# A transformer block on one core: the array's work cut into blocks of two matmuls, and an opening with the identity made on chip

## The chip, the core and the metric

The kernel runs on one core of a Trainium2 chip. The metric is the device time of one execution in microseconds (us), lower is better. The engines are TensorE (PE, "the array"; its weight loads are PEld), VectorE (DVE), ScalarE (ACT), GpSimd (POOL) and SyncE (SP), which issues most DMAs. Each engine takes its instructions in order; they meet through semaphores.

## What is computed

Input x is 2048 x 1024 (S x D), everything in bfloat16. The reference, cut to its core:

```python
h  = x + _A_ref(_layernorm(x), A_wqkv, A_wo)
h2 = h + _B_ref(_layernorm(h), B_w_in, B_w_sp, B_b_sp, B_w_out)

# _A_ref: 32 heads of 32, each position attends to itself and 7 earlier ones, 2 apart
idx = pos[:, None] - (jnp.arange(8) * 2)[None, :]
logits = einsum('bhsd,bhswd->bhsw', q, k[idx]) * scale       # masked where idx < 0
o = einsum('bhsw,bhswd->bhsd', softmax(logits), v[idx]) @ wo

# _B_ref
z = gelu(x @ w_in);  z1 = z[..., :1792];  z2 = _layernorm(z[..., 1792:])
g = einsum('ts,bsf->btf', w_sp, z2) + b_sp[None, :, None]
return (z1 * g) @ w_out
```

## The kernel before

The sequence is worked on in four chunks of 512 positions (`NCH`, `CH`), each of four tiles of 128 rows (`TPC`, `P`). The matrix products run on the array with 128 x 128 weights and up to 512 columns, and collect in PSUM tiles `acc` of two banks, of which there are three. The stages, in the array's order:

- **The opening** (L208 to L359) handles the first chunk before anything else can run. Eleven matmuls on a zeroed tile warm the array up (L212). Tiles 0 and 1 of x arrive in halves on SP's and ACT's queues (L222); behind them ACT's queue issues the constants `csb` (L223), and SP the eight pieces of the Q weights (`wq`, L225), with tiles 2 and 3 of x in between (L228), then the further pairs of x tiles (L206), K's weights (L231) and V's (L238). For each tile: VectorE computes the statistics (L242 to L244), ACT the root (L266), VectorE the reciprocal (L317) and the normalized tile in pieces (`norm`, L272, `cuts`); the array transposes it in blocks of 128 columns against the identity (`xpose`, L283), and ACT copies the result out of PSUM (L284). The Q projection (`q_mm`, L287) follows: one row block of weights (`kt`) at a time, eight matmuls for one tile (`q_left`).
- **The constants** `csb` are one tile of 416 columns that a DMA brings: the identity (128), two 0/1 matrices for the attention, `E32` and `B4`, and a mask.
- **The planned part** (L372 to L889): the projections of K and V for the first chunk and of all three for the others (`qkv`, L439), attention (VectorE products L497 to L507 and L610 to L621, with small matmuls at L527 and L589), the output projection `head` (L684), the two halves of the MLP input, `b_z2` (L761) and `b_z1` (L816).
- **The end**, in fixed order: the spatial product (L912), then the output projection (L927) and the store.

The order of the planned part is worked out when the program is built. `Order` (L64) is a list scheduler: each operation has an engine, a cost in us, dependences, a priority and sometimes a slot to take or free (`acc` has 3). The engine that is free first takes the ready operation of lowest priority number. An operation of better priority that isn't ready is waited for if the wait is under 0.3 of the candidate's cost. The planner starts its engines at fixed clocks: PE 22.9, ACT 24.1, DVE 15.4 and POOL 12.0 us. What comes out is an instruction order for each engine; on the chip the engines follow that order and wait for each other by semaphores alone.

The array's work is handed to the planner in blocks of four matmuls of 512 columns, 0.8634 us each. In `qkv` and `b_z1` a PSUM tile of two halves takes four blocks (`PIECES`: half `j`, starting at weight block `k0`); in `head` and `b_z2` a tile takes four parts of two `dl` or `kt` steps with two matmuls each. In `b_z2`'s second half a step has 512 and 256 columns, and the block costs 0.650.

The opening's first lines of work, where tiles 0 and 1 are handled:

```python
    xn[0] = norm(0, cuts=(0, 2 * P, CH, D))
    for put in [xpose(0, lo, hi, tag) for lo, hi, tag in ((0, 2, "t0"), (2, 4, "t1"), (4, 8, "acc"))]:
        put(A.copy)
    qacc.extend((new_acc(), new_acc()))
    stats(V, 1)
    scale(1)
    xn[1] = norm(1, cuts=(0, CH, D))
    q_left(0, ALONE - 1, 0, 1)
    xpose(1, 0, 4, "t0")(A.copy)
    q_left(ALONE - 1, ALONE, 0, 1)
    xpose(1, 4, 8, "t1")(A.copy)
```

`ALONE` is 5: tile 0 alone goes through five of the eight weight blocks, four of them ahead of tile 1's first transposes and one between its two groups. GpSimd's first computing instruction is a power for the second chunk's normalization (L405).

Of the kernel before, what the change touches and what calls it, by code (L numbers as in the profile page):

```python
# [20 lines left out]
P = 128  # L21
NT = S // P
CH = 512
# [13 lines left out]
LSLACK, BSLACK = 2.0, 0.3  # L37
Z2ACT = (4, 4, 4, 0)
L2DVE = (0, 0, 2)
PIECES = ((0, 0), (0, 4), (1, 0), (1, 4))  # L40
LNPRIO = (0, 2.0, 2.5, 2.8)
LAST_COLS = ((0, 512), (512, 896), (896, 1024))


def _consts():
    c = np.zeros((P, 128 + 32 + 128 + 128), np.float32)
    c[:, 0:128] = np.eye(P)
    for p in range(P):
        c[p, 128 + p // 4] = 1.0
    for k in range(P):  # L50
        h = k % 32
        c[k, 160 + 4 * h:160 + 4 * h + 4] = 1.0
    for w in range(W_WIN):
        for s in range(16):
            if s - DIL * w < 0:
                c[0:32, 288 + w * 16 + s] = NEG
    return c.astype(ml_dtypes.bfloat16)


# [68 lines left out]
def kernel(  # L128
# [28 lines left out]
    z2_d = dpool.tile([S, FH], BF16, name="z2_d")  # L157

    cpool = ctx.enter_context(tc.tile_pool(name="consts", bufs=1))
    csb = cpool.tile([P, 416], BF16, name="csb")  # L160
    ident = csb[:, 0:128]
    E32 = csb[:, 128:160]
    B4 = csb[:, 160:288]
    maskb = csb[0:32, 288:416].rearrange("p (w s) -> p w s", w=W_WIN)
    eps_t = cpool.tile([P, 1], FP32, name="eps_t")
    texp = cpool.tile([P, 1], FP32, name="texp")
    nhalf = cpool.tile([P, TPC], FP32, name="nhalf")
# [42 lines left out]
    wps = ps_tp.tile([P, CH], FP32, name="wps", tag="t0")  # L210
    for _ in range(NWARM):
        T.matmul(wps[:], warm[:, 0:P], warm[:], start=True, stop=True)  # L212
    V.memset(eps_t[:], EPS)
    V.memset(nhalf[:], -0.5)

    wsb = [wtile([P, KT, D], "wq", "wA"), wtile([P, KT, D], "wk", "wA"), wtile([P, KT, D], "wv", "wB")]
    with tc.manual_schedule(engines={mybir.EngineType.SP}):
        for i in range(TPC):
            x_slot(i)
        for i in range(2):  # L220
            for q_, lo in ((nc.sync, 0), (nc.scalar, CH)):
                q_.dma_start(xts[i][:, lo:lo + CH], x2d[i * P:(i + 1) * P, lo:lo + CH])  # L222
        A.dma_start(csb[:], consts_d.ap()[:, :])  # L223
        for kt in range(KT):
            dma(wsb[0][:, kt, :], wq_view[:, kt, 0:D])  # L225
            if kt == 4:
                for i in (2, 3):
                    dma(xts[i], x2d[i * P:(i + 1) * P, :])  # L228
        load_pair(2)
        load_pair(3)  # L230
        dma(wsb[1][:], wq_view[:, :, D:2 * D])  # L231
        load_pair(4)
        load_pair(5)
        xl = att.tile([P, TPC, D], BF16, name="xl", tag="prod", bufs=2)
        dma(xl[:], x2d[3 * CH:4 * CH, :].rearrange("(t p) d -> p t d", p=P))
        for i in range(TPC):
            xts[3 * TPC + i] = xl[:, i, :]
        dma(wsb[2][:], wq_view[:, :, 2 * D:3 * D])  # L238
# [38 lines left out]
    xns = {c: bp.tile([P, TPC, D], BF16, name=f"xns{c}", tag=f"hn{c - 1}", bufs=1) for c in (1, 2)}  # L277

    def xpose(i, lo, hi, tag):
        ps = (ps_acc.tile([P, 2, 2 * CH], BF16, name="tpa", tag="acc")[:, 0] if tag == "acc" else  # L280
              ps_tp.tile([P, 2 * CH], BF16, name="tp" + tag, tag=tag))
        for a in range(lo, hi):
            T.transpose(ps[:, (a - lo) * P:(a - lo + 1) * P], xn[i][:, a * P:(a + 1) * P], ident)  # L283
        return lambda cp: cp(xnT[0][:, i, lo:hi, :], ps[:, 0:(hi - lo) * P].rearrange("p (a s) -> p a s", s=P))  # L284

    def q_mm(dst, dl, kt, lo, hi, start, stop):
# [33 lines left out]
    A.activation(wsq[:], eps_t[:], ACTF.Sqrt)  # L320
    stats(V, 0)
    scale(0)
    xn[0] = norm(0, cuts=(0, 2 * P, CH, D))
    for put in [xpose(0, lo, hi, tag) for lo, hi, tag in ((0, 2, "t0"), (2, 4, "t1"), (4, 8, "acc"))]:
        put(A.copy)
    qacc.extend((new_acc(), new_acc()))
    stats(V, 1)
    scale(1)
    xn[1] = norm(1, cuts=(0, CH, D))
    q_left(0, ALONE - 1, 0, 1)  # L330
    xpose(1, 0, 4, "t0")(A.copy)
    q_left(ALONE - 1, ALONE, 0, 1)
    xpose(1, 4, 8, "t1")(A.copy)
    stats(V, 2)
    sd2 = root(2, 3)
    st3 = stats_half(3, 0)
# [32 lines left out]
        dma_w(t[:], win_view[:, :, c0:c0 + wd])  # L369
        wins[k] = t  # L370

    o_ = Order({"PE": 22.9, "ACT": 24.1, "DVE": 15.4, "POOL": 12.0}, {"acc": 3, "L": 1, "prod": 1, "part": 2, "xn": 4})  # L372
    add = o_.add
    G = {}

# [52 lines left out]
    def qkv(c):  # L428
        for xi in range(0 if c else 1, 3):
            wv = wsb[xi][:].rearrange("p kt (m dl) -> p kt dl m", dl=DLO)  # L430
            for dp in range(DLO // 2):
                key = ("acc", "qkv", c, xi, dp)
                deps = [G.get(("xnT", c))]
                for j, k0 in PIECES:
                    def mm(j=j, k0=k0, dl=2 * dp + j, wv=wv, key=key):
                        if j == 0 and k0 == 0:
                            G[key] = new_acc()
                        for kt in range(k0, k0 + 4):
                            T.matmul(G[key][:, j, :].rearrange("p (a b) -> p a b", a=TPC), wv[:, kt, dl, :], xnT[c][:, :, kt, :],  # L439
                                     start=(kt == 0), stop=(kt == KT - 1))  # L440
                    last = add("PE", 0.8634, mm, deps, prio=order(), take="acc" if j == 0 and k0 == 0 else None)
                    deps = [(last, 0.0)]
                def ev(xi=xi, dp=dp, key=key):
                    if c == 0:
                        A.copy(att_in[0][xi][:, 2 * dp:2 * dp + 2, HALO:HALO + CH], G[key][:])
                        if dp == 3:
                            dma(qkv_d[xi][:, :, CH - HALO:CH], att_in[0][xi][:, :, CH:CH + HALO])
                    else:
                        stg = l1.tile([P, 2, CH], BF16, name="stg", tag="xn", bufs=4)
                        A.copy(stg[:], G[key][:])  # L450
                        dma(qkv_d[xi][:, 2 * dp:2 * dp + 2, c * CH:(c + 1) * CH], stg[:])
                G["ev", c, xi, dp] = add("ACT", 0.92, ev, [last], prio=2.0, free="acc", lat=0.15, take="xn" if c else None)
                if c:
                    dma_op(3.5, lambda: None, [G["ev", c, xi, dp]], free="xn")
            G["wdone", c, xi] = last
        G["qkvlast", c] = last
# [3 lines left out]

    def attention(c):
        if c == 0:
            d_q = add("DMA", 24.2, lambda: None)
            d_k, d_v = G["ev", 0, 1, 3], G["ev", 0, 2, 3]
        else:
            def ld(which):
# [195 lines left out]
    def head(c):  # L662
# [6 lines left out]
        for il in range(TPC):  # L669
            i = c * TPC + il  # L670
            deps = [G["avdone", c]]
            for part in range(4):
                def mm(part=part, il=il, i=i):
                    if part == 0:
                        if il == 0:
# [3 lines left out]
                            for k in range(min(XRB, TPC)):  # L679
                                xr_load(k)  # L680
                        st["acc", il] = new_acc()
                    for dl in range(2 * part, 2 * part + 2):
                        for nh in range(2):
                            T.matmul(st["acc", il][:, nh, :], oTs[c][:, dl, il * P:(il + 1) * P], wo_sb[:, dl, nh * CH:(nh + 1) * CH],  # L684
                                     start=(dl == 0), stop=(dl == DLO - 1))
                def xr_load(k):
                    st["xr", k] = bp.tile([P, D], BF16, name="xr", tag="xr", bufs=XRB)
                    dma(st["xr", k][:], x2d[(c * TPC + k) * P:(c * TPC + k + 1) * P, :])
                m_ = add("PE", 0.8634, mm, deps, prio=prio + il * 1e-2 + part * 1e-3, take="acc" if part == 0 else None)
                deps = [(m_, 0.0)]  # L690
            def res(il=il, i=i):
                hb = st["hnc"][:, il, :]
# [49 lines left out]
    def b_z2(c):  # L742
        st = {}
        sqd = []
        for il in range(TPC):
            evs = []
            for hf in range(2):
                wd = win_specs[hf][1]
                deps = [G.get(("hnT", c, il), G["hnT", c]), G["win", hf]]
                for part in range(4):  # L750
                    def mm(part=part, hf=hf, il=il, wd=wd):
                        if part == 0:
                            st["acc"] = G["accz", c, il, hf] = new_acc()
# [1 line left out]
                                st["sums"] = bp.tile([P, TPC, 2], FP32, name="sums", tag="sums")  # L755
                                st["sqs"] = bp.tile([P, TPC], FP32, name="sqs", tag="sqs")
                        accf = G["accz", c, il, hf][:].rearrange("p a b -> p (a b)")
                        for kt in range(2 * part, 2 * part + 2):
                            for n0 in range(0, wd, CH):
                                n1 = min(n0 + CH, wd)  # L760
                                T.matmul(accf[:, n0:n1], hnTs[c][:, il, kt, :], wins[hf][:, kt, n0:n1],  # L761
                                         start=(kt == 0), stop=(kt == KT - 1))
                    m_ = add("PE", 0.8634 if hf == 0 else 0.650, mm, deps, prio=order(), take="acc" if part == 0 else None)
                    deps = [(m_, 0.0)]
                def ev(hf=hf, il=il, wd=wd):
                    if hf == 0:
# [39 lines left out]
    def b_z1(c):  # L806
        for fp in range(NF // 2):
            deps = [G["hnT", c], G["win", 2 if fp < 4 else 3]]
            for j, k0 in PIECES:
                def mm(j=j, k0=k0, fp=fp):  # L810
                    f = 2 * fp + j
                    wt, f0 = (wins[2], f) if f < 8 else (wins[3], f - 8)
                    if j == 0 and k0 == 0:
                        G["accy", c, fp] = new_acc()
                    for kt in range(k0, k0 + 4):
                        T.matmul(G["accy", c, fp][:, j, :].rearrange("p (a b) -> p a b", a=TPC), wt[:, kt, f0 * P:(f0 + 1) * P],  # L816
                                 hnTs[c][:, :, kt, :], start=(kt == 0), stop=(kt == KT - 1))
                m_ = add("PE", 0.8634, mm, deps, prio=order(), take="acc" if j == 0 and k0 == 0 else None)
                deps = [(m_, 0.0)]
            def ev(fp=fp):  # L820
                z1s = l1.tile([P, 2, CH], BF16, name="z1s", tag="xn", bufs=4)
# [151 lines left out]
```

## Time and profile before

| | |
|---|---|
| three runs | 724.37 us median, 724.16 to 726.34 |
| the profiled execution's own time | 723.34 us |
| its span, first to last instruction | 721.6 us |
| PE busy | 714.1 us, 99% of the span |
| DVE busy | 420.8 us, 58% |
| ACT busy | 217.7 us, 30% |
| POOL busy | 51.2 us, 7% |
| warm-up matmuls (L212) | 1.19 to 5.32 us |
| first transpose (L283) | 6.31 us |
| first Q matmul (L287) | 7.04 us |
| first matmul of tile 1 (L287) | 10.13 us |
| first K matmul (L439) | 23.07 us |

The profile is of one execution, and its times count from the first instruction. The page gives the busy time of each engine, its share in 40 slices of the span, and the chain that ended last: the last instruction, what released it, and so on back to the start. Other views give the same chain in order of time, the instructions of a line, the waits of an engine and the DMAs with their time from issue to landing. In a row of the waits the three numbers are the total in us, the count and the longest.

### The profile page before, as it was taken

How to read it: one execution, taken by the hardware profiler on the slowest of the kernel's cores; microseconds unless marked ns; L12 is line 12 of the kernel's file. 1: busy time of each engine (PE TensorE's matmuls, PEld its weight loads, DVE VectorE, ACT ScalarE, POOL GpSimd, SP SyncE). 2: the span in 40 equal slices, each digit the busy share in tenths (PEclk: the TensorE clock that was granted, in tenths of full speed). 3: DMA queues.
4: the chain of work that ended last, by engine and by line, in shares of the span. 5: the costliest groups of instructions: out<-in, count | busy, mean ns of one | idle time of the engine just before them, and what ended most of it. 6: DMA issues, size and time to landing. Idle time of an engine off the chain costs nothing.

```text
span 721.6 us, 8559 instructions
## 1 busy us (share of the span) xinstructions
PE 714.1 (99%) x3493; PEld 370.3 (51%) x3537; DVE 420.8 (58%) x470; ACT 217.7 (30%) x280; POOL 51.2 (7%) x61
## 2 busy tenths in 40 slices
PE   8999999999999999999999999999999999999998
PEld 7766665666545444445445444444444444444444
DVE  6899899999999799988951103222222222222222
ACT  4523432533348866738825420000000000000000
POOL 0100010012110111000204100000000000000000
PEclk9999999999999999999999999999999999999999
DMA  9964697389973594642849899163016411120002
GB/s 327 322 185 110 201 215 206 128 233 277 312 301 58 188 238 142 233 117 66 223 129 294 230 299 295 48 148 116 29 45 128 132 33 45 35 86 11 0 17 71
DMA packets 117590, 113.12 MB, mean 157 GB/s; under 512 B 68080, under 2 KB 95120, under 8 KB 117424
## 3 DMA queue, kind: packets, MB, share of 16 engines
q1 hardware_dynamic: 108528, 75.48, 35.7%
q0 software_dynamic: 8448, 36.64, 17.6%
q8 instruction: 27, 0.44, 0.3%
q10 hardware_dynamic: 576, 0.47, 0.2%
q14 instruction: 11, 0.09, 0.0%
HBM read 57.19 MB, written 31.26 MB: 123 GB/s over the span
## 4 chain that ended last, share of the span: by engine, by line
PE 98%; DMA 0%; DVE 0%; issue 0%; ACT 0%
PE acc L912 27%; PE acc L439 21%; PE acc L816 13%; PE acc L761 13%; PE acc L927 13%; PE acc L684 8%; PE acc L287 2%; DMA xp<-in_A_x_dram 0%; PE L L527 0%; PE tpt L283 0%; PE pb L589 0%; DVE bnst L242 0%; DVE xn L272 0%; DVE bnst L243 0%; PE tpa L283 0%
## 5 line engine op out<-in xcount | busy, mean ns | idle before, releaser
L912 PE MATMUL acc<-wspT,z2sb 128*128 128x512 bf16 x878 | 193.1, 379 | 0.9
L912 PEld LDWEIGHTS <-z2sb 128*128 128x128 bf16 x896 | 87.7, 98 | 105.7
L915 DVE TENSOR_TENSOR g<-acc,bB 128x1024 bf16<-128x1024 f32 x28 | 34.3, 1224 | 160.2 <-PE acc L912 127.9
L816 PE MATMUL acc<-hnT,win 128*128 128x512 bf16 x448 | 98.0, 379 | 0.0
L761 PE MATMUL acc<-win,hnT 128*128 128x512 bf16 (+1 forms) x501 | 97.4, 352 | 0.6
L761 PEld LDWEIGHTS <-hnT 128*128 128x128 bf16 x512 | 49.9, 98 | 47.5 <-issue 0.7
L497 DVE TENSOR_TENSOR prod<-qT,kT 128x4096 bf16<-128x4096 bf16 x32 | 72.4, 2283 | 0.0
L927 PEld LDWEIGHTS <-zg 128*128 128x128 bf16 x462 | 44.7, 98 | 52.4
L816 PEld LDWEIGHTS <-win 128*128 128x128 bf16 x448 | 43.7, 98 | 52.6 <-issue 0.7
L450 ACT CAST stg<-acc 128x1024 bf16<-128x1024 f32 x36 | 36.4, 1011 | 77.2 <-PE acc L439 66.4
L934 DVE TENSOR_TENSOR ot<-acc,hr 128x1024 bf16<-128x1024 f32 x15 | 18.4, 1225 | 69.4 <-PE acc L927 60.5
L927 PE MATMUL acc<-wout_a,zg 128*128 128x512 bf16 (+2 forms) x260 | 58.0, 373 | 0.3
L439 PE MATMUL acc<-xnT,wk 128*128 128x512 bf16 x256 | 56.5, 380 | 0.0
L439 PE MATMUL acc<-xnT,wv 128*128 128x512 bf16 x256 | 56.1, 380 | 0.0
L684 PE MATMUL acc<-wo_sb,av_oT 128*128 128x512 bf16 x250 | 55.6, 379 | 0.3
L439 PEld LDWEIGHTS <-wv 128*128 128x128 bf16 x256 | 36.7, 144 | 18.5 <-issue 0.2
L439 PEld LDWEIGHTS <-wk 128*128 128x128 bf16 x256 | 36.6, 144 | 18.7 <-issue 0.7
L927 PE MATMUL acc<-wout_b,zg 128*128 128x512 bf16 (+2 forms) x193 | 43.8, 373 | 0.2
L439 PE MATMUL acc<-xnT,wq 128*128 128x512 bf16 x192 | 42.1, 380 | 0.0
L684 PEld LDWEIGHTS <-av_oT 128*128 128x128 bf16 x256 | 25.0, 98 | 30.1
L822 ACT ACTIVATE z1s<-acc 128x1024 bf16<-128x1024 f32 x28 | 28.6, 1022 | 37.8 <-PE acc L816 33.5
L501 DVE TENSOR_TENSOR prod<-prod 128x2048 bf16<-128x2048 bf16 x32 | 38.4, 1217 | 0.1
(140 smaller groups left out, 562.1 us busy)
## 6 DMA issues: line engine op xcount, KB each, us to landing
qkv_d<-stg SPq DMA_DIRECT2D x36, 256.0 KB, 3.9
z_d<-z1s SPq DMA_DIRECT2D x28, 256.0 KB, 2.6
z1c<-z_d SPq DMA_DIRECT2D x28, 256.0 KB, 2.8
z_d<-u SPq DMA_DIRECT2D x12, 448.0 KB, 2.8
z2sb<-z_d POOLq DMA_DIRECT2D x12, 448.0 KB, 9.7
xr<-in_A_x_dram SPq DMA_DIRECT2D x16, 256.0 KB, 3.1
av_y<-av_z POOLq DMA_DIRECT2D x4, 1024.0 KB, 8.6
av_oT<-av_zz POOLq DMA_DIRECT2D x4, 1024.0 KB, 12.1
```

The costliest lines, as they stand in the source:

```text
L439: T.matmul(G[key][:, j, :].rearrange("p (a b) -> p a b", a=TPC), wv[:, kt, dl, :], xnT[c][:, :, kt, :], start=(kt == 0), stop=(kt == KT - 1))
L450: A.copy(stg[:], G[key][:])
L497: V.tensor_tensor(st["prod"][:], qT[:], kT[:, :, o:o + CH], op=ALU.mult)
L501: V.tensor_tensor(dst, p_[:, 0:4, :], p_[:, 4:8, :], op=ALU.add)
L684: T.matmul(st["acc", il][:, nh, :], oTs[c][:, dl, il * P:(il + 1) * P], wo_sb[:, dl, nh * CH:(nh + 1) * CH], start=(dl == 0), stop=(dl == ...
L761: T.matmul(accf[:, n0:n1], hnTs[c][:, il, kt, :], wins[hf][:, kt, n0:n1], start=(kt == 0), stop=(kt == KT - 1))
L816: T.matmul(G["accy", c, fp][:, j, :].rearrange("p (a b) -> p a b", a=TPC), wt[:, kt, f0 * P:(f0 + 1) * P], hnTs[c][:, :, kt, :], start=(kt ...
L822: A.activation(z1s[:], G["accy", c, fp][:], ACTF.Gelu_apprx_tanh)
L912: T.matmul(acc[:, j, :], z2sb[a][:, f * P:(f + 1) * P], wspT[:, a, :], start=(a == 0), stop=(a == NT - 1))
L915: V.tensor_tensor(g1[:], acc[:], bB[:, c * CH:(c + 1) * CH].unsqueeze(1).to_broadcast([P, 2, CH]), op=ALU.add)
L927: T.matmul(outs, zg[:, f, il * P:(il + 1) * P], wt[:, f0, lo:hi], start=(f == 0), stop=(f == NF - 1))
L934: V.tensor_tensor(ot[:], acc[:].rearrange("p a b -> p (a b)"), hr[:], op=ALU.add)
```

## The change

It has two parts. In the first, the blocks that the planner gets for the array hold two matmuls of 512 columns instead of four, at 0.4317 us (0.325 in `b_z2`'s second half); the matmuls themselves, their order within a PSUM tile and their number stay. In the second, the opening is changed:

- The identity is a tile of its own. GpSimd sets it to zero and writes the ones on the diagonal with `affine_select`. `csb` is left with 288 columns.
- The DMA of `csb` moves from ACT's queue, where it followed the first x halves, to SP's, behind the eighth piece of `wq`.
- Tile 0 is normalized, transposed and copied in pieces of 128, 256 and 640 columns instead of 256, 256 and 512. The first eight Q matmuls of tile 0 stand ahead of the transposes of its third piece.
- Tile 1 is cut into 256 and 768 columns instead of 512 and 512. All five weight blocks of tile 0 come ahead of its transposes, with no Q matmuls between its two groups.
- The planner's clocks are 22.4 for PE and 23.6 for ACT, and Q is counted as there at 23.7 instead of 24.2.

```diff
-PIECES = ((0, 0), (0, 4), (1, 0), (1, 4))
+PIECES = tuple((j, k0) for j in range(2) for k0 in range(0, 8, 2))
...
-    csb = cpool.tile([P, 416], BF16, name="csb")
-    ident = csb[:, 0:128]
+    csb = cpool.tile([P, 288], BF16, name="csb")
+    ident = cpool.tile([P, P], BF16, name="ident")
...
+    nc.gpsimd.memset(ident[:], 0.0)
+    nc.gpsimd.affine_select(out=ident[:], in_=ident[:], compare_op=ALU.not_equal, fill=1.0, base=0, pattern=[[-1, P]], channel_multiplier=1)
...
-        A.dma_start(csb[:], consts_d.ap()[:, :])
         for kt in range(KT):
             dma(wsb[0][:, kt, :], wq_view[:, kt, 0:D])
...
+        dma(csb[:], consts_d.ap()[:, :])
         load_pair(2)
...
-    xn[0] = norm(0, cuts=(0, 2 * P, CH, D))
-    for put in [xpose(0, lo, hi, tag) for lo, hi, tag in ((0, 2, "t0"), (2, 4, "t1"), (4, 8, "acc"))]:
-        put(A.copy)
+    xn[0] = norm(0, cuts=(0, P, 3 * P, D))
+    xpose(0, 0, 1, "t0")(A.copy)
+    xpose(0, 1, 3, "t1")(A.copy)
+    tpa = ps_acc.tile([P, 2, 2 * CH], BF16, name="tpa", tag="acc")
     qacc.extend((new_acc(), new_acc()))
+    q_left(0, 1, 0, 1)
+    xpose(0, 3, 8, "acc")(A.copy)
     stats(V, 1)
     scale(1)
-    xn[1] = norm(1, cuts=(0, CH, D))
-    q_left(0, ALONE - 1, 0, 1)
-    xpose(1, 0, 4, "t0")(A.copy)
-    q_left(ALONE - 1, ALONE, 0, 1)
-    xpose(1, 4, 8, "t1")(A.copy)
+    xn[1] = norm(1, cuts=(0, 2 * P, D))
+    q_left(1, ALONE, 0, 1)
+    xpose(1, 0, 2, "t0")(A.copy)
+    xpose(1, 2, 8, "t1")(A.copy)
...
-    o_ = Order({"PE": 22.9, "ACT": 24.1, "DVE": 15.4, "POOL": 12.0}, {"acc": 3, "L": 1, "prod": 1, "part": 2, "xn": 4})
+    o_ = Order({"PE": 22.4, "ACT": 23.6, "DVE": 15.4, "POOL": 12.0}, {"acc": 3, "L": 1, "prod": 1, "part": 2, "xn": 4})
...
-                        for kt in range(k0, k0 + 4):
+                        for kt in range(k0, k0 + 2):
...
-                    last = add("PE", 0.8634, mm, deps, prio=order(), take="acc" if j == 0 and k0 == 0 else None)
+                    last = add("PE", 0.4317, mm, deps, prio=order(), take="acc" if j == 0 and k0 == 0 else None)
...
-            for part in range(4):
+            for part in range(8):
```

`head` and `b_z2` are cut in the same way (eight parts of one `dl` or `kt` step), and `b_z1` like `qkv`.

## The prediction

> **What bounds the kernel now.** The page comes first: its span, its engines, the slices, the chain by engine.
>
> ```profile
> span 721.6 us, 8559 instructions
> ...
> PE 714.1 (99%) x3493; PEld 370.3 (51%) x3537; DVE 420.8 (58%) x470; ACT 217.7 (30%) x280; POOL 51.2 (7%) x61
> ...
> PE   8999999999999999999999999999999999999998
> ...
> PE 98%; DMA 0%; DVE 0%; issue 0%; ACT 0%
> ```
>
> TensorE is busy 714.1 of 721.6 us, and 98% of the chain that ends last is its own work. Next, all waits of TensorE (engine, line, what it waited for: us in total, times, longest):
>
> ```profile
> PE wps L212 <- DVE eps_t L213: 1.2, 1, 1.2
> PE tpt L283 <- DVE xn L272: 1.0, 1, 1.0
> ```
>
> The first ends with the warm-up's start, the second before the first transpose. Behind that the array stalls a little more before 10.17 us, and then not again. A microsecond lost in the opening is therefore a microsecond at the end, and elsewhere there is hardly one to gain. The chain in order of time (start, length) shows the opening:
>
> ```profile
> 5.66 0.61 DVE xn L272 x2
> 6.28 0.04 issue
> 6.31 0.38 PE tpt L283 x4
> 6.70 0.35 PE tpa L283 x4
> 7.04 0.00 issue
> 7.04 2.09 PE acc L287 x32
> 9.13 0.33 PE tpt L283 x4
> 9.46 0.49 PE acc L287 x8
> 9.94 0.22 PE tpt L283 x4
> 10.17 3.41 PE acc L287 x48
> ```
>
> VectorE is named as the releaser of 6.31, wrongly: the first normalized piece, 0.35 us from 5.66, ends at 6.01. The weight-load sequencer's own row, from the view of line 283, tells who was late:
>
> ```profile
> L283 PEldq EVENT_SEMAPHORE  x1: 51/51/51, 6.2 to 6.2; - x1
> ```
>
> And the list of DMA issues (KB each, us from issue to landing):
>
> ```profile
> csb<-qt_consts ACTq DMA_DIRECT2D x1, 104.0 KB, 4.5
> ```
>
> The constants, issued at 1.68, land at 6.18; the sequencer's wait ends there. So the identity held the first transpose by some 0.28 us, and the change does remove that wait. What it puts in its place is the question.
>
> **The blocks of two matmuls** add no instruction and take none away. They let the planner put a ready operation into the array's order up to 0.43 us sooner. The array has no hole for that to fill (the waits above), so the gain is 0. The loss is bounded by what the array meets early. Between VectorE's result and the array's first instruction on it there are now, in the four rounds of attention: 0.92, 0.51, 0.50 and 1.44 us (L507 to L527); 1.31, 0.77, 0.36 and 1.36 (L570's first half to L589); 0.94, 0.28, 0.62 and 1.51 (L621 to L684). If the array came 0.43 us sooner at each, with 0.05 for a semaphore, it would stall 0.12 and 0.20 us, 0.3 in all; a whole old block sooner (0.86), 2.4 us. Two adjoining facts speak for the low end: blocks are halved, not removed, and the array already runs 0.2 us behind its planner clock (22.9 against 23.07). I take 0, and keep 0.3 in the range.
>
> **The late constants.** The 72 KB copy now stands on SP's queue behind the last piece of wq; each issue there takes about 0.45 us, and the two load pairs, wk and the rest are issued behind it. They are not waiting for SP: wk is issued at 8.63 and lands at 21.36, far behind in the stream of 380 to 400 GB/s, and is needed at 23.07. Cover 1.7 us, cost 0; without the cover, 0.45. The first user of the constants is L532's or L527's work at 75 us. Without the old 104 KB the wq pieces land up to 0.27 us sooner (104 KB at 390 GB/s); they have 0.5 us to spare or more already (the second lands at 6.61 for 7.53), so 0. SP held the sixth piece until 6.19, as the constants landed; it now goes sooner, for a use at 12.54. ACT's queue loses one issue of 0.45 us at 1.68, and ACT then idles until 5.13 either way: 0.
>
> **The opening, if the identity is there.** Durations: norm pieces 0.35 us at 256 columns and 0.41 at 512, hence 0.31 at 128; ACT copies 0.37 at 256 and 0.59 at 512, hence 0.27 at 128; a transpose starts every 0.056 us and ends 0.22 after its start; a Q matmul every 0.060; hand-overs 0.03 to 0.05. Call R the start of the first transpose. Its result is copied by R + 0.22 + 0.04 + 0.27, and the first 8 Q matmuls start 0.05 later, at R + 0.58. They take 0.48, the five transposes behind them 0.28, the 32 further matmuls 1.92: tile 1's transposes at R + 3.26. There the order has lost its filler: before, 8 matmuls stood between tile 1's two groups and covered the copy; now tile 1's first matmul waits for two transposes (0.056 + 0.22), 0.04, the copy 0.37 and 0.05, so it starts at R + 4.00. Now it starts at 10.13, with the same work behind it. Change = R + 4.00 - 10.13 = **R - 6.13**.
>
> The earliest R is the 128-column piece's end at 5.97 plus some 0.06: 6.03, a gain of 0.10 us. Tile 1's root waits behind the 640-column copy (ends near 8.27) and not the statistics (8.06), which puts its first piece at 9.04; the array asks at 9.29, so it is hidden. With none of the new stalls the gain would be 0.40; that is its bound.
>
> **The identity's price** is the unknown term. GpSimd gets a memset and a select. Four memsets run from 0.24 us at 0.10 us each. The select has no row; the nearest are 0.10 (memset) and 1.04 (L405), and I take 0.5. But something stands ahead of GpSimd's first computing instruction:
>
> ```profile
> L405 POOLq MODIFY_POOL_CONFIG  x2: 8/10/11, 0.8 to 0.8; - x2
> L405 POOL TENSOR_TENSOR rstd<-ve,nhalf x1: 1037/1037/1037, 20.8 to 20.8; 128x4 f32<-128x4 f32 x1
> ```
>
> Two reconfigurations at 0.75 and 0.78, carried by L405's line, and then nothing until 20.83. The memsets ran before them. I read the pair as setting up code that the computing instructions need; the select becomes the first of these. How long the set-up takes the trace hides: between 0 and the 20.0 us until L405, which starts without delay. Bounds for R - 6.13 are thus -0.10 and, at 20.8 + 0.5, over 15 us. Nearest rows: if code is fetched from memory, it shares the opening's traffic, where x halves take 3.1 us from issue to landing and the constants 4.5. Two such steps in turn: 0.79 + 3.1 + 4.5 = 8.39, with the select 8.89, R = 8.92, change **+2.79**. I take that, as there are two records. One step alone, at 2.8 to 5.9 us (the first load and the pair issued at 7.51), gives 4.1 to 7.2 and R 6.03 to 7.2.
>
> The Trainium skill (GPSIMD Engine Reference, Instruction dispatch) says that GpSimd's kernels are loadable and that the first call after such a load pays about 6 us (5.95 measured) which no profiled instruction shows. By that, as an estimate, the identity would be there at 0.78 + 5.95 + 0.5 = 7.2 and the change would be +1.1. No row here times the load; the two records at 0.75 and 0.78 are all that this trace has of it.
>
> A second part of the price is the clock. The warm-up's matmuls start every 0.43 us until 4.51 and every 0.216 from then on, with the granted clock given as 1.00 throughout. They end at 5.32. With R = 8.92 the array idles 3.6 us instead of 0.99. If it falls back to the slow rate for as long as at the start (3.3 us), half of that is lost, 1.65. No row has such a gap, so I take 0 and keep 1.65 above. The Trainium skill (TensorE: Matmul & The Clock Gate, Part 1: The HAM clock gate) says that an idle window of some 3.4 us brings the half rate back; by that rule this gap is on the edge, and the forecast would be +4.4.
>
> **Sum** against the profiled execution, 723.34 us (span 721.6 and 1.74 around it): blocks 0, constants 0, opening +2.79, so 726.13. The runs' median is 724.37, 1.03 above; by it the forecast is **727.2**.
>
> **Rivals.**
> 1. The identity is on time (not slower): the select needs nothing of the pair, or the pair is quick. For it: the records last 0.01 us, and GpSimd is otherwise idle until 20.83. It decides at 5.97: any end before that gives -0.10, 724.3; with the bound 0.40, 724.0. Chance 0.21.
> 2. One step of loading, with the identity near 7.2: R = 7.23, +1.1, 725.5. The load then delays the array by its excess over 5.97 alone; its length is the upper end of one step above. The rule of the Trainium skill (GPSIMD Engine Reference, Instruction dispatch) gives this case. Chance 0.13.
> 3. Two steps, the forecast: 725.8 to 729.0, 727.2. Chance 0.48.
> 4. A longer set-up with the clock lost: the kernel's planner counts GpSimd from 12.0 us; there R = 12.5, +6.4 and +1.65 make 732.4, and in between lies 729 to 732.4. Chance 0.13.
> 5. The blocks stall the array at the hand-overs on top of rival 1: 0.3 to 2.4 us, 724.6 to 726.7. For it: margins of 0.28 and 0.36; against it: the halved block. Chance 0.03.
> 6. Something faster than the bound of 0.40: no row gives it. Chance 0.02.
>
> **Numbers.** A measurement of this kernel tells about 0.3% (2.17 us, so 722.2 to 726.5) from no change. Slower by more: the forecast but for 0.04 of it that ends below 726.5, rival 4, and 0.01 of rival 5: 0.58. Faster: 0.02. Within: 0.40. The range 723.9 to 730.0 leaves out the longer half of rival 4, rival 6 and the edge of rival 1, some 0.15; the forecast's own range is 725.8 to 729.0.
>
> **What would show it.** In the changed kernel, GpSimd's select: its start and end against 5.97. An end before it and a first transpose at 6.03 refute the forecast, and tile 1's first matmul at 10.03 would then confirm the rest. With a late one, the first transpose follows the select within 0.1 us, tile 1's first matmul follows 4.0 us behind, and the clock shows in the first Q matmuls' spacing, 0.060 or 0.12. The waits of TensorE after that should stay empty; entries at L527, L589 or L684 would mean rival 5. K's first matmul (L439), now at 23.07, carries the sum of the opening.

## The result and the profile after

| | before | after |
|---|---|---|
| median of 22 executions | 723.89 us | 729.12 us |
| lowest to highest | 723.19 to 726.34 | 723.52 to 734.54 |
| the profiled execution's own time | 723.34 us | 731.0 us |
| its span | 721.6 us | 729.2 us |
| first transpose | 6.31 us | 5.81 us |
| first matmul of tile 1 | 10.13 us | 9.82 us |
| first K matmul | 23.07 us | 22.77 us |

The ratio is 1.0054 (95% interval 1.0040 to 1.0068): slower, by half a percent. The ratios follow the mean, not the median, and leave out executions over 1.5% above their kernel's fastest (734.54 here, 736.9 and 737.7 below). The times after are spread: 6 of the 22 lie at 723.5 to 724.7, as before, the other 16 at 725.9 to 734.5. So something goes wrong in most executions and not in all; what spares the six is not shown, as one execution was profiled. The forecast of 727.2 (723.9 to 730.0) holds the median, but, as the next views show, not for its reason.

The page of the kernel after:

```profile
span 729.2 us, 8560 instructions
...
PE 716.8 (98%) x3493; PEld 370.6 (51%) x3537; DVE 421.1 (58%) x470; ACT 217.6 (30%) x280; POOL 52.5 (7%) x63
...
PE   9999999999999999999999997999999999999998
...
PE 93%; DMA 4%; SPq 1%; issue 1%; DVE 1%; ACT 0%; DVEq 0%
```

The first slice, where the forecast put its loss, is better than before (9, was 8). The dent is the 7 in the 25th slice, 437 to 456 us. The chain is no longer TensorE's alone: 4% of it are DMAs, 1% SP's queue. TensorE's waits after:

```profile
PE acc L913 <- DVE g L916: 4.8, 1, 4.8
PE wps L211 <- DVE eps_t L214: 1.2, 1, 1.2
PE acc L762 <- DMA hnT<-hb: 0.6, 1, 0.6
...
```

The wait of 1.0 us at the first transpose is down to 0.2. New are one wait at the z2 matmuls (L762) and one at the spatial matmul (L913), both far behind the opening. Next GpSimd's timeline in the first 3 us (start, length):

```profile
0.74 0.20 POOL L212 MEMSET ident<- 128x128 bf16 x1 [0.29 <-POOLq L958]
1.02 0.29 POOL L213 TENSOR_SCALAR_AFFINE_SELECT ident<-ident 128x128 bf16<-128x128 bf16 x1
```

The two reconfigurations are there, now at 0.89 and 0.92 by GpSimd's queue, and the select starts 0.09 us behind the second. The identity is ready at 1.31 us, 4.5 us ahead of its first use. The chain in order of time shows the opening that follows:

```profile
5.81 0.24 PE tpt L284
...
6.40 0.65 PE acc L288 x8
...
9.82 3.46 PE acc L288 x48
...
```

And the same view shows where the loss is (375 to 460 us; before, this stretch of the chain was TensorE's alone). `hnT` is the normalized input of the MLP, which a DMA transpose turns for each tile of 128 rows. A spatial transpose (`wspT`) turns the 512 rows of `w_sp` that a chunk needs. The row bias is `b_sp`:

```profile
381.82 16.73 DMA hnT<-hb
...
398.60 6.23 PE acc L762 x32
404.83 24.17 PE acc L817 x112
...
429.27 6.65 PE acc L913 x30
435.92 4.50 SPq L835
...
443.32 4.57 DMA z_d<-z1s
...
448.16 0.34 SPq L902
...
449.04 4.21 DMA z1c<-z_d
...
453.27 1.24 DVE g L916
...
454.55 2.29 PE acc L913 x5
```

To be read from the top: the last hnT transpose of chunk 3 takes 16.73 us and the z2 matmuls wait for it. Later SP's queue stands in the spatial transpose of L835 until 440.4, the last z1 stores behind it land at 447.9, the row bias (L902) and the first z1 pieces read back (L908) come behind those, VectorE frees its PSUM tile only then, and the array waits. The chain names a z1 piece as the last to land, but VectorE's instruction (L916) reads the sums and the row bias alone. The row bias landed at 452.95 and it started at 453.27; in three more profiles (before, and the two below that move the row bias or the z1 stores to ScalarE's queue) it starts 0.31 or 0.32 us behind the row bias as well.

The sizes, from the starts of the matmuls: 0.79 us more than usual at 397.7 and 4.99 at 449.3. Behind the second gap of 5.2 us the spacing is 0.427 instead of 0.216 from 454.55 to 459.1: eleven steps in 4.54 us that should take 2.37, another 2.17. With the opening, 0.30 us sooner at the first K matmul, they make 7.65, against 7.66 between the two profiled executions.

**What moved.** The DMAs from 379 us on, read from the trace:

| issue to landing, us | before | after |
|---|---|---|
| third hnT transpose | 381.71 to 384.90 | 379.41 to 382.48 |
| last z1 store of chunk 2 | 381.25 to 383.57 | 381.09 to 383.36 |
| first of twelve z2 loads | 383.68 to 387.69 | 381.57 to 386.14 |
| fourth hnT transpose | 383.87 to 389.98 | 381.82 to 398.55 |
| second z2 load | 384.33 to 390.05 | 382.22 to 398.48 |
| last z2 load lands | 402.60 | 409.58 |
| first spatial transpose lands | 412.87 | 420.81 |
| output weights land | 424.5, 428.9 | 438.2, 442.4 |
| second spatial transpose holds SP's queue until | 433.73 | 440.43 |
| row bias lands | 443.27 | 452.95 |

The store is issued when ScalarE has done the last gelu of z1 in chunk 2. Before, the planner wrote that gelu ahead of the head's last square (starts 380.20 and 381.12); with blocks of two it wrote it behind (380.06 and 379.00). ScalarE's timeline before and after (L698 and L700 are the square):

```profile
380.20 1.02 ACT L822 ACTIVATE z1s<-acc 128x1024 bf16<-128x1024 f32 x1 [1.95 <-issue]
381.12 1.05 ACT L698 ACTIVATE xr<-hb 128x1024 bf16<-128x1024 bf16 x1
```

```profile
379.00 1.06 ACT L700 ACTIVATE xr<-hb 128x1024 bf16<-128x1024 bf16 x1 [2.35 <-issue]
...
380.06 1.00 ACT L823 ACTIVATE z1s<-acc 128x1024 bf16<-128x1024 f32 x1
```

So the fourth transpose moves up by 2 us and meets the store still in flight beside the z2 loads. Before, it had only the loads beside it (list of DMA issues at 383 to 386 us):

```profile
hnT<-hb SPq DMA_TRANSPOSE x1, 6.1
```

The rest of the table follows from edges in the program. The first spatial transpose waits for all twelve z2 loads, and the output weights wait for that transpose. The second spatial transpose starts at 418 to 419 us in both kernels, so weights that are issued at 421.4 instead of 413.5 fall on nearly the whole of it.

The swap is not the only one: the whole change moves about a dozen operations of ScalarE against before, the first at 75 us, and issues of SP's queue with them. My theory from here: **the blocks alone do the loss, by that one swap in the written order, through the DMA queues**. Rivals: another of the swaps does it; the opening does it (its timing shifts everything by tenths); the blocks do it through the array itself; or the row bias is late for a reason of its own.

### The profile page after: what moved, and what is told of

It reads as the page before. It is cut to its first block, busy times and chain, and to the rows that moved or that the text cites. A ratio compares the mean times of both kernels' runs of the same rounds, so it can differ in the third digit from the quotient of the medians.

```text
span 729.2 us, 8560 instructions
## 1 busy us (share of the span) xinstructions
PE 716.8 (98%) x3493; PEld 370.6 (51%) x3537; DVE 421.1 (58%) x470; ACT 217.6 (30%) x280; POOL 52.5 (7%) x63
## 4 chain that ended last, share of the span: by engine, by line
PE 93%; DMA 4%; SPq 1%; issue 1%; DVE 1%; ACT 0%; DVEq 0%
PE acc L913 25%; PE acc L442 21%; PE acc L928 13%; PE acc L817 13%; PE acc L762 11%; PE acc L686 8%; DMA hnT<-hb 2%; PE acc L288 2%; DMA z_d<-z1s 1%; SPq L835 1%; DMA z1c<-z_d 1%; SPq L824 0%; DMA xp<-in_A_x_dram 0%; DMA h_d<-hb 0%; PE L L530 0%
## 5 line engine op out<-in xcount | busy, mean ns | idle before, releaser
L913 PE MATMUL acc<-wspT,z2sb 128*128 128x512 bf16 x878 | 195.3, 382 | 5.9 <-DVE g L916 4.8
L913 PEld LDWEIGHTS <-z2sb 128*128 128x128 bf16 x896 | 88.2, 98 | 112.4 <-issue 8.1
L916 DVE TENSOR_TENSOR g<-acc,bB 128x1024 bf16<-128x1024 f32 x28 | 34.3, 1224 | 167.4 <-PE acc L913 126.0
L762 PE MATMUL acc<-win,hnT 128*128 128x512 bf16 (+1 forms) x501 | 97.6, 352 | 1.2 <-DMA hnT<-hb 0.6
L762 PEld LDWEIGHTS <-hnT 128*128 128x128 bf16 x512 | 49.9, 98 | 48.4 <-DMA hnT<-hb 1.0
L686 PE MATMUL acc<-wo_sb,av_oT 128*128 128x512 bf16 x250 | 55.6, 379 | 0.3
L686 PEld LDWEIGHTS <-av_oT 128*128 128x128 bf16 x256 | 25.0, 98 | 30.0
L769 ACT ACTIVATE u<-acc 128x1024 bf16<-128x1024 f32 (+1 forms) x32 | 29.3, 915 | 33.5 <-PE acc L762 33.5
```

Source lines behind the costliest of these rows:

```text
L686: T.matmul(st["acc", il][:, nh, :], oTs[c][:, part, il * P:(il + 1) * P], wo_sb[:, part, nh * CH:(nh + 1) * CH], start=(part == 0), stop=( ...
L762: T.matmul(accf[:, n0:n1], hnTs[c][:, il, part, :], wins[hf][:, part, n0:n1], start=(part == 0), stop=(part == KT - 1))
L769: A.activation(st["u", il][:, hf * 1024:hf * 1024 + wd], G["accz", c, il, hf][:].rearrange("p a b -> p (a b)")[:, 0:wd], ACTF.Gelu_apprx_t ...
L913: T.matmul(acc[:, j, :], z2sb[a][:, f * P:(f + 1) * P], wspT[:, a, :], start=(a == 0), stop=(a == NT - 1))
L916: V.tensor_tensor(g1[:], acc[:], bB[:, c * CH:(c + 1) * CH].unsqueeze(1).to_broadcast([P, 2, CH]), op=ALU.add)
```

## The experiments

Each was timed beside the kernel before on one chip; "before" is its median there.

**One part alone.** First the whole opening with blocks of four, then the blocks of two with the old opening. Of the first, one line against the whole change (the cuts of `head`, `b_z2` and the loops go back likewise):

```diff
-PIECES = tuple((j, k0) for j in range(2) for k0 in range(0, 8, 2))
+PIECES = ((0, 0), (0, 4), (1, 0), (1, 4))
```

> The changed opening with the old blocks of four matmuls (planner clocks as in the change). Theory A (the blocks move the last transpose of hnT, 381.82 to 398.55 in the changed kernel, into the z2 loads and the last z1 store, and everything behind it comes late): the last transpose lands within 8 us of its issue as before, no wait of the array at the spatial product, K's first matmul at 22.9, median 723.2 to 724.2. Rival B (the opening, which brings the late part of the program about 0.15 us forward in the array and the constants behind wq, is what moves the DMAs): median 727 to 731 as with the whole change, the last transpose over 12 us.

723.67 us (12 executions, 723.23 to 724.02; before 723.43), ratio 0.9989 (0.9977 to 1.0001); fourth transpose 6.1 us. The second kernel is the reverse, the change's first part alone:

> The blocks of two matmuls with the old opening, old constants and old planner clocks. Theory A: as with the whole change, single runs between 723.5 and 734 and a median of 726 to 731, the last transpose 10 to 17 us, the array waiting 3 to 5 us for L915's sums at the spatial product. Rival B: 723.5 to 724.3, within 0.1% of before.

732.47 us (12 executions, two at 723.3, the others 728.5 to 736.9), ratio 1.0088 (1.0056 to 1.0120). Its waits:

```profile
PE acc L910 <- DVE g L913: 7.2, 1, 7.2
PE tpt L283 <- DMA csb<-qt_consts: 1.8, 1, 1.8
```

The same late wait, and a fourth transpose of 13.9 us. The loss is the blocks'; the opening costs nothing. (The second row is a side matter taken up below; in this execution it adds 1.5 us to the start of K, so the ratio is not the late wait's alone.)

**Is it the collision?** The whole change, with the first z2 load held until the fourth transpose has landed:

```diff
+            if i == 0:
+                tc.add_manual_dep(zl[0].ins, G["hnTdma", TPC - 1].ins.name, wait_for, reason="keep the z2 loads out of the last transpose")
```

> The whole change, with the first of the twelve z2 loads held back until the last hnT transpose has landed, so that the two do not share the DMA engines. Theory A: the transpose lands in 2.5 to 3.5 us (the three before it took 3.0), the z2 loads, 1.12 us each, end near 400, wspT's first transpose starts about 10 us sooner than in the changed kernel (409.7), no wait of the array behind 10 us, and all runs within 1 us of 723.5: the opening's gain of 0.15 to 0.3 us is left, 723.3 to 723.8. Rival C (the z2 loads are slow by themselves, or the transpose is slowed by the z1 store that is issued 0.7 us ahead of it, not by the loads): the transpose still takes over 8 us in some runs and the median stays over 725.

723.46 us (723.03 to 724.01; before 723.43), ratio 0.9986 (0.9971 to 1.0000). From the list of DMA issues at 382 to 385 us:

```profile
hnT<-hb SPq DMA_TRANSPOSE x1, 3.0
```

3.0 us, with the store issued 0.75 us ahead of it as in the whole change. Both new waits are gone. The z2 loads start 4.7 us later (386.29) and yet the last lands 5.5 us sooner (404.08). ScalarE and SP's queue run in the order of the whole change here, so its other swaps cost nothing.

**Which partner?** The same order, the z2 loads free, but the store held until the transpose has landed:

```diff
+                        tc.add_manual_dep(last_store[0].ins, t4.ins.name, wait_for, reason="keep the store out of the last transpose")
```

> The whole change with its order, but the last z1 store of chunk 2 waits until the fourth hnT transpose has landed; the z2 loads still start a quarter of a microsecond ahead of that transpose. Theory A (the store in flight is what makes the collision worse than before's): the fourth transpose takes about 6 us as before, time about 723.5. Theory B (the z2 loads alone, issued just ahead, do it, and before escaped by the timing of a few tenths): still 13 to 17 us and 729 us in most executions. Theory C (the transpose waits for its turn in a queue behind the store): 3 us.

723.45 us (722.90 to 724.09; before 723.62), ratio 0.9996 (0.9988 to 1.0005). The same row:

```profile
hnT<-hb SPq DMA_TRANSPOSE x1, 6.1
```

That is Theory A. With the store alone beside it the transpose takes 3.0 us, with the z2 loads alone 6.1 (as in the kernel before, where the store had landed 0.3 us ahead of it), with both 14 to 17 in six profiles. Why the three together are so much worse than two stays open.

**Is it the order, or the size of the blocks?** Blocks of four in z1 alone, or in qkv alone, bring ScalarE's old order back at 380 us; in the head alone they do not, as the traces of the three kernels show. Each is the whole change with blocks of four in one kind of work.

> The whole change, but the z1 matmuls of all four chunks stay in blocks of four; qkv, head and z2 keep blocks of two. With that the written order on ScalarE puts the last z1 gelu of chunk 2 ahead of the last square of the head's chunk 3 again, as before the change. Theory (that order decides, because it moves the last z1 store beside the last hnT transpose): the store issues ahead of the third hnT transpose again, the fourth takes about 6 us from issue to landing and not 14 to 17, no stall of 4 us or more at the spatial matmul, and the time is that of before, 723.4 to 723.9 us. Rival (any of the blocks of two brings the loss, through the array's timing and not through that order): 728 to 732 us, as with the whole change.

723.58 us (723.30 to 724.17; before 723.62), ratio 0.9996 (0.9987 to 1.0004); fourth transpose 6.4 us.

> The whole change, but the K and V of chunk 0 and the qkv of the later chunks stay in blocks of four; z1, z2 and head keep blocks of two. The matmuls at the place of the loss (z1 and z2 of chunks 2 and 3) are thus in blocks of two, but the written order on ScalarE again has the last z1 gelu of chunk 2 ahead of the last square of the head. Theory (the order decides, not the size of a block): the store issues ahead of the third hnT transpose, the fourth takes about 6 us, time 723.3 to 723.9. Rival (blocks of two in z1 as such cost): 728 us or over.

723.47 us (11 executions, 723.10 to 723.77; before 723.51), ratio 0.9998 (0.9990 to 1.0007); 6.2 us.

> The whole change, but the head's matmuls stay in blocks of four. The written order on ScalarE keeps the last z1 gelu of chunk 2 behind the last square, as in the whole change. Theory (order): the last z1 store lies between the third and fourth hnT transposes, the fourth takes 13 us or more, and most executions are at 727 to 732 us. Rival (the number of blocks ahead of the array as such, in whichever part): in between, 724 to 727.

730.78 us (11 executions, two under 725, the others 727.0 to 737.7), ratio 1.0084 (1.0056 to 1.0112). Its wait and its transpose, in two views:

```profile
PE acc L915 <- DVE g L918: 5.5, 1, 5.5
```

```profile
hnT<-hb SPq DMA_TRANSPOSE x1, 15.4
```

All three as the written order says. In the qkv kernel z1, z2 and the head are in blocks of two at the place of the loss, ScalarE and SP's queue run throughout in the order of the kernel before (but for the constants' load), and nothing is lost: here a block's size as such is harmless to the array. In the head kernel both run in the order of the whole change, and the loss is there. No run changes the one swap and nothing else.

**The links behind it.** The row bias and the first z1 pieces on ScalarE's queue (the bias's line is shown):

```diff
-    dma(bB[:], B_b_sp.unsqueeze(0).to_broadcast([P, S]))
+    A.dma_start(bB[:], B_b_sp.unsqueeze(0).to_broadcast([P, S]))
```

> The whole change, with the DMAs of bB and of the first chunk's z1c on ACT's queue instead of SP's, where they stand behind wspT's second transpose (419.04 to 440.43 at SP in the changed kernel) and the z1 stores. The collision is left as it is. Theory A, second link (the array's 5.0 us wait at 449 is SP's queue being held by that transpose, not the late data as such): bB lands before 440, the wait at 449 goes and with it the slow clock behind it, median 723.5 to 725.5 with what is left of the wait for hnT at 397.7 (0.8 us). If the z2 loads' own lateness or the wspT data set the end, the median stays at 727 to 731.

A miss: 729.57 us (6 executions, 728.62 to 730.07), ratio 1.0067 (1.0047 to 1.0088). The row bias was issued at 447.06 from its new queue, 0.2 us after the last z1 store had landed (446.88). So it waits for the stores themselves, not for its place in the queue; and the stores stand behind the spatial transpose. Two kernels take that link apart. First the output weights, held until the second spatial transpose has landed (their loads are also written behind it; the changed edge is shown):

```diff
-        tc.add_manual_dep(i_.ins, wsp_ins[0].ins.name, wait_for, reason="keep the load out of the xbar transpose")
+                        tc.add_manual_dep(i_.ins, wsp_ins[1].ins.name, wait_for, reason="keep the load out of the xbar transpose")
```

> The whole change, but both loads of the output weights wait until the second spatial transpose has landed, where they waited for the first. It leaves the collision of the fourth hnT transpose with the z2 loads (13 to 17 us, 0.5 to 1 us of waiting at the z2 matmuls). Theory (second link: the weight loads beside the second spatial transpose make it 21 to 26 us where it was 15.6, and SP's queue holds the last z1 stores behind it): that transpose takes about 15.6 us, the stores issue by about 437, the row bias lands by 443 to 445, the wait of 5 us at the spatial matmul goes, and the time is 724 to 725 us. Rival (the late first link alone sets the row bias, whatever the weight loads do): the wait stays at 3 us or more and the time at 727 or over.

723.41 us (723.14 to 724.42; before 723.62), ratio 0.9989 (0.9978 to 0.9999). The second spatial transpose in SP's timeline (start, time that it holds the queue), after and in this kernel:

```profile
419.04 21.39 SPq L835 DMA_TRANSPOSE wspT<-in_B_w_sp_dram  x1
```

```profile
418.24 7.94 SPq L835 DMA_TRANSPOSE wspT<-in_B_w_sp_dram  x1
```

The collision is still there (14.1 us for the fourth transpose, last z2 load at 407.8), but the transpose holds the queue 7.9 us instead of 21.4, the stores follow at 426 and the wait at the spatial matmul is gone. I had expected 15.6, the value of the kernel before; that one already overlapped with the weights. Then the last z1 stores on ScalarE's queue:

```diff
-                last_store[:] = [dma(z1_d[2 * fp:2 * fp + 2, :, c * CH:(c + 1) * CH].rearrange("f p s -> p f s"), z1s[:])]
+                last_store[:] = [(A.dma_start if c == NCH - 1 else dma)(z1_d[2 * fp:2 * fp + 2, :, c * CH:(c + 1) * CH].rearrange("f p s -> p f s"), z1s[:])]
```

> The whole change, but the z1 stores of chunk 3 are issued from ScalarE's queue, so that the second spatial transpose on SP's queue has none of them behind it. The collision stays (fourth transpose 13 to 17 us) and so does the slowing of the second spatial transpose beside the output weights (it lands at 440 to 445). Theory (third link: the row bias is late because the stores stand behind that transpose in SP's queue, and it waits for their landing): the row bias issues right behind the transpose, at about 441, lands by 446, the wait at the spatial matmul shrinks from 4.8 to at most 1 us, time 723.5 to 725. Rival (the row bias and the chunks read back would be late anyway, because they stand behind the same transpose): the wait stays at 3 us or more, 727 us or over.

Half right: 724.44 us (723.47 to 731.92), ratio 1.0032 (1.0008 to 1.0056). In its profiled execution (723.47) the row bias is issued at 441.23 and lands at 446.75, with no wait of the array, and seven of the twelve lie under 724.5; but four lie at 728.7 to 731.9. What holds those is open; the second spatial transpose still ends at 440.9 here, and all that is read back stands behind it.

**Where the opening's gain is.** The kernel before has executions of 725 to 727 us, 23 of 120 over the four sets of runs. Does its own mild collision cause them?

> The kernel before, with the first z2 load held until the last hnT transpose has landed. Theory (the collision is already in the kernel before, only milder: 6.1 us instead of 3, inside its cover): median unchanged, 723.3 to 723.6, and the executions of 725 to 727 us that the kernel before shows now and then are gone. Rival (the later z2 loads cost something of their own, since every later transpose moves with them): 724.5 or over.

No: 723.89 us (723.28 to 726.19), ratio 1.0001 (0.9987 to 1.0015), and five of twelve still at 725.3 or over. The profiled one took 725.28, and its chain tells why:

```profile
1.67 5.27 DMA csb<-qt_consts
...
7.07 0.59 PE tpt L283 x4
...
8.09 3.07 PE acc L287 x32
...
12.10 3.42 PE acc L287 x48
```

The constants land at 6.94 instead of 6.18 and hold the first transpose until 7.07. Behind it the 32 Q matmuls take 3.07 us where they took 2.09: they start every 0.107 us until 10.55 and every 0.06 from 10.62 on. Tile 1 starts 1.93 us later than in the profile of before, and the execution is 1.94 us longer. Then the identity alone, with the constants left where they were:

```diff
-    ident = csb[:, 0:128]
+    ident = cpool.tile([P, P], BF16, name="ident")
```

> The kernel before with one part of the opening alone: the identity is made on GpSimd; the constants keep their place and size and tile 0 its cut. Theory (the executions of 725 to 727 us that the kernel before shows, about three in ten, are those in which the constants' transfer lands late and holds the first transpose, as in two profiles of kernels with the old opening, 1.0 and 1.8 us): first transpose at 5.8 to 6.3, median 723.3 to 723.7 and none of twelve executions over 724.6. Rival (those executions come from elsewhere, from the collision of the z2 loads or from the landing of x): three or four of twelve at 725 or over, as before.

Inconclusive: 723.42 us, ten of eleven at 723.25 to 724.13 and one at 725.9; before had but 3 of 34 over 725 on that chip. Its constants landed at 5.65, so its profile says nothing either.

## Why the prediction was right or wrong

- **What bounds the kernel**: right. The array bounds it before and after, and every wait of it is time at the end.
- **The blocks, "I take 0"**: this step failed. The array indeed gained and lost nothing from them at the hand-overs (no entry of TensorE's waits at L530, L592 or L686 after; rival 5 did not come). But I followed the blocks on the array alone. They are also the planner's grain: with them it wrote, among other moves that cost nothing, two operations of ScalarE the other way round, and that moved a store and a transpose on SP's queue by 2 us against each other. The blocks alone measured 1.0088. The bound of 0.3 to 2.4 us was for the wrong place. The views that could have told were in the profile of before: a fourth transpose that took 6.1 us where the others took 3, with the first of twelve loads issued 0.19 us ahead of it.
- **The late constants, 0**: right. wk landed at 21.18 for a first K matmul at 22.77.
- **The opening's formula, R + 4.00**: near. From R = 5.81 it gives 9.81; measured 9.82. In the other nine profiles with the new opening tile 1 starts between 0.01 us sooner and 0.44 later than it says. R itself was put at 6.03 at the earliest. It came at 5.81 because x landed 0.22 us sooner in that execution, but in seven of the ten profiles it is 6.0 to 6.2: there all eleven warm-up matmuls started 0.43 us apart and ended at about 6.0. Once the identity is early, the warm-up's end is mostly late next; the prediction had not asked that. In these seven tile 1 starts at 10.19 to 10.67, where it started at 10.13 before, which fits an opening that is worth next to nothing in the median.
- **The identity's price, ready at 8.89**: this step failed, and it was the whole forecast. Measured 1.31. The pair of reconfigurations is followed by the select within 0.09 us. The rule of the Trainium skill (GPSIMD Engine Reference, Instruction dispatch) of some 6 us before the first call to freshly loaded code does not show here: the select, GpSimd's first instruction behind the pair, starts at once, and nothing in the trace says that the pair loads code. Two records of 0.01 us were read as a price; the bound from below, "nothing", was the right end.
- **The clock, 0 with 1.65 kept**: not put to the test, as the late identity that would have opened the gap did not come. The rate fell where no one looked: 2.17 us were lost at half rate behind the 5.2 us gap at 449, none behind the gap of 0.8 us at 397.7. Two executions with the old opening and late constants show that the length of a gap does not settle it: with 1.0 us of waiting the array ran at half rate until 10.6, with 1.8 us its transposes started every 0.055 us at once.
- **The sum**: 727.2 lay near 729.12 by accident. Rival 1's condition held for the opening: alone it lies 0.24 us above the median of before on its chip (723.67 and 723.43), where rival 1 had 0.10 below. No rival had the loss that came. "Slower" was right for a wrong reason.

A kernel that keeps both parts without the loss needs one edge in the order: z2 loads behind the transpose (723.46), or the store behind it (723.45), or the weights behind the second spatial transpose (723.41). Against the median of before that is within what can be told. What it does bring is steadiness: in the six kernels with the new opening and without the late wait, 0 of 71 executions are over 724.5, against 25 of 120 before; the means are 723.53 and 724.05. That the late constants made those executions is shown for one profile, not for all, and which part of the opening removes them is not settled.

## What to carry to other kernels

A change to the grain of a planner is a change to the order of every queue that it feeds: compare the written orders of all engines and DMA queues first, and look at each pair of operations that swap. A transfer that takes twice its siblings' time in the profile of before is a warning of a collision with little room. A record of next to no length is no price: where only its start is known, the bound of nothing is as near as any other.

## What the runs showed of the hardware

- A transpose of 128 by 1024 through the DMA takes 3.0 us beside one 256 KB store, 6.1 to 6.4 beside the 448 KB loads, 14 to 17 beside both, and in that case the loads beside it stall too: the second z2 load landed at 398.5, not at 390. The second spatial transpose holds SP's queue 7.9 us with no load of weights beside it, 15.6 with part of their 3.5 MB (before) and 21.4 with all of it (after); the z1 stores behind it in that queue were issued as it ended, at 426, 434 and 440.5.
- With the same eleven warm-up matmuls from 1.19 us in every kernel, the rise to full rate came at 4.0 us in two profiles (row bias on ScalarE's queue; blocks of four in qkv), at 4.5 before, at 5.0 after, and in the other ten not before the last warm-up matmul, which started at 5.4. In the execution with constants that landed at 6.94 it came at 10.6; in the one where they landed at 7.77 the array was at full rate at 7.90. The Trainium skill (TensorE: Matmul & The Clock Gate, Part 1: The HAM clock gate) has a window of some 3.4 us that runs freely, one busy window giving the full rate and one idle window the half; by that rule the rise varies with the window's phase. The profiles agree, as far as rises at 4.0 to 10.6 us can show it.
